# A written order for every engine in the late stage of an attention and FFN kernel

## The chip, the cores and the metric

The kernel runs on one core of one Trainium2 chip. The metric is the device time of one execution in microseconds (us). TensorE, the matrix engine, is PE in the profile, VectorE is DVE, ScalarE is ACT, GpSimd is POOL and SyncE, whose queue issues nearly all the transfers of this kernel, is SP.

## The reference

Windowed attention over 8 batches, 8 heads, 576 tokens and a head size of 64, and behind it a feed-forward network on the 4608 tokens, all in fp32:

```python
def _attn_ref(q, k, v):
    scores = scale * np.matmul(q, k.transpose(0, 1, 3, 2))
    ...
    scores = np.where(masks[None, :, :, :], scores, -1000000000.0)
    scores = scores - np.max(scores, axis=-1, keepdims=True)
    attn = np.exp(scores)
    attn = attn / (np.sum(attn, axis=-1, keepdims=True) + 1e-09)
    return np.matmul(attn, v)

def _moe_ref(x, w_in, w_out):
    h = x @ w_in                                                 # 4608x512 @ 512x2048
    g = np.maximum(h, 0.0) + np.log1p(np.exp(-np.abs(h)))        # softplus
    return g @ w_out                                             # 4608x2048 @ 2048x512
```

Half of the heads see the last 32 tokens, the other half every fourth of the last 128.

## The kernel before

**Chunks.** The 4608 tokens are taken in 9 chunks of 512 (`CH`). For each chunk the attention is computed in four groups of two heads (`Group`, numbered j = 0 to 3); their outputs, transposed, are the chunk's x (512 features by 512 tokens). Then come x @ w_in, softplus and the product with w_out. Fp32 products are made of three matmuls on fp32r parts: every operand is split into a high part (a cast, on ScalarE) and a low part (the value minus its high part, on VectorE).

**Three stages.** An opening, written out step by step by hand (`OPENING`), starts chunks 0 and 1; a middle stage does the rest of them in 32 slots, one tile of 128 hidden features by 512 tokens each (`h_part`, `o_part`). The late stage, chunks 2 to 8 (`FIRST = 2`), takes two hidden tiles at a time: it replaces the eight block products of a pair of tiles by seven, of sums and differences of blocks of x and of w_in. A chunk has 8 pairs (p0 to p7), and a pair has 7 steps (k0 to k6, the table `steps`). A step is one product of six matmuls 128x256 into one of two PSUM banks, h_x for k0, k2, k4, k6 and h_y for k1, k3, k5; then one sum on VectorE that takes the product out of PSUM (`aside`, lines 831 and 833; called "the aside" below); then `outputs`: one group of three matmuls 128x512 of the product with w_out, two groups after k6. The first two pairs of the late stage have 6 output groups each and not 8 (`between`), so the outputs run 12 groups behind: in the second pair (p1) of every chunk from 3 on, the four banks o_ps0 to o_ps3 get the last groups of the chunk before in k0 to k3, and the first groups of the new chunk in k4, k5 and, both, k6 (o_ps2, then o_ps3). Between those, the finished bank is copied out: o_ps1 and o_ps3 by ScalarE (line 865), o_ps0 and o_ps2 by VectorE (line 867).

**The other work of the late stage.** With a full hidden tile, ScalarE does Abs, Exp and Ln (lines 545 to 547, `activated`), VectorE the maximum with 0 and the sum (`softplus`, line 552), ScalarE the high part gh (line 567), VectorE the low part gl (line 573). The last tile halves of a pair come with the asides of k5 and k6. For the attention of the next chunk there are the scores on PE (s_ps), scaling, mask and maximum on VectorE (lines 347 and 350), eight exponentials on ScalarE (line 356), the divisor on VectorE (368, 371), the division on POOL (374), a transpose in squares on VectorE (407) whose result SP sends to DRAM and brings back in three pieces (turned<-squares, pt<-turned, line 132), and the values on PE (a_ps), copied to x_full by ScalarE (470). When a chunk's x is there, its block sums are made (`combine`, line 255) and the seven blocks are split into high and low parts (`split`, lines 270 and 271). In chunk 2, the last two of eight pairs of w_in tiles are converted to the late stage's form (`convert`, lines 696 to 714).

**Chunk 1's outputs** are accumulated in two runs. The sum of the first run is in DRAM (kept) and is loaded into ob tiles (line 590), which take the memory of chunk 2's block sums; the second run's PSUM banks are added to them (line 615) in p1 of chunk 2.

**What sets the order.** Matmuls and the loads made by `load_dma` keep the order of the program on their engines. So does all that goes through `pin` while `opening` is true, that is in the opening. Everywhere else the order on VectorE, ScalarE and POOL, and of the transfers issued with a plain `dma_start`, is chosen by the framework's scheduler from a simulated timeline. `at(when, ...)` puts a step of the attention or of the conversion into a list of events, and `pump(now)` issues those that are due. In the late stage one unit of `when` is one hidden tile, so a pair takes two.

## Time and profile before

| | |
|---|---|
| time, median of 3 runs | 907.86 us (906.24 to 909.62) |
| own time of the profiled execution | 907.07 us |
| its span, from the first to the last instruction | 905.3 us |
| PE busy | 879.8 us (97%) |
| VectorE busy | 634.9 us (70%) |
| ScalarE busy | 542.0 us (60%) |
| POOL busy | 64.1 us (7%) |
| mean granted clock of PE | 0.998 |
| first aside of the late stage / of chunk 8 | 238.48 us / 809.38 us |

The span is the time between the first and the last instruction; the execution's own time has what lies around it too. A row of the timeline gives the start of an instruction or of a run of like ones, how long it is busy, its engine, line, operation, the tiles it writes and reads, and their number; in brackets stands the idle time of the engine just before it and whose end it waited for. On PE matmuls overlap, so a matmul of 0.40 us may have the next one start 0.23 us after it. For SP the time is that of issuing; the data land later.

### The profile page before, as it was taken

The page shows a single profiled execution, that of the slowest core. Times are in us where ns is not written, and L with a number is a line of the kernel's source. Part 1 is how long each engine was busy: PE and PEld are TensorE (multiplying, and loading weights), DVE is VectorE, ACT ScalarE, POOL GpSimd, SP SyncE. Part 2 cuts the span into 40 slices and gives each one's busy share as a digit, 9 for nine tenths or more (in the row PEclk, how much of TensorE's full clock was granted, in tenths as well). Part 3 has the DMA queues.
Part 4 walks back from the last instruction along what each step waited for, and adds up shares of the span by engine and source line. Part 5 has one row for each costly group of instructions (what it writes and reads, how often), then busy time and mean ns, then how long its engine had stood idle before and what let it go on. Part 6 is the DMA issues. An engine that isn't in the chain of part 4 may idle for free.

```text
span 905.3 us, 18339 instructions
## 1 busy us (share of the span) xinstructions
PE 879.8 (97%) x6972; PEld 742.3 (82%) x6978; DVE 634.9 (70%) x1242; ACT 542.0 (60%) x1348; POOL 64.1 (7%) x46
## 2 busy tenths in 40 slices
PE   6899999999999999999999999999999999999998
PEld 3567888788788888888888888888888888889987
DVE  4799998997696586657666675668665866575444
ACT  6677677775555576556555665556555655564443
POOL 1320000000000000000000001000000000000000
PEclk9999999999999999999999999999999999999999
DMA  9989334333555546554555446545654455424223
GB/s 295 315 277 375 131 135 155 129 104 107 190 171 162 163 141 217 170 162 156 198 183 180 161 159 203 185 147 171 203 166 157 166 200 164 152 94 158 98 94 117
DMA packets 79095, 156.41 MB, mean 173 GB/s; under 512 B 8864, under 2 KB 21792, under 8 KB 79008
## 3 DMA queue, kind: packets, MB, share of 16 engines
q1 hardware_dynamic: 78432, 154.18, 51.2%
q8 instruction: 55, 0.90, 0.4%
q10 hardware_dynamic: 576, 1.07, 0.3%
q14 instruction: 32, 0.26, 0.1%
HBM read 124.28 MB, written 30.93 MB: 171 GB/s over the span
## 4 chain that ended last, share of the span: by engine, by line
PE 79%; DVE 12%; ACT 5%; DMA 2%; issue 2%; ACTq 0%; SPq 0%; DVEq 0%
PE o_ps L189 37%; PE h_x L189 17%; PE h_y L189 12%; PE h_ps L189 7%; PE a_ps L189 3%; ACT s L356 2%; PE s_ps L189 2%; DVE e L552 1%; DVE gl L573 1%; DVE s L347 1%; ACT e L547 1%; DMA k<-kpl 1%; DVE nm L350 1%; DMA out_t<-ob 1%; DVE a L162 1%
## 5 line engine op out<-in xcount | busy, mean ns | idle before, releaser
L189 PE MATMUL o_ps<-gh,t 128*128 128x512 f32 (+1 forms) x904 | 341.6, 391 | 0.0
L189 PEld LDWEIGHTS o_ps<-gh,t 128*128 128x128 f32 x904 | 169.7, 188 | 21.4
L189 PE MATMUL o_ps<-gl,t 128*128 128x512 f32 (+1 forms) x452 | 178.3, 394 | 0.0
L545 ACT ACTIVATE e<-hs 128x512 f32<-128x512 f32 x112 | 69.9, 629 | 162.2 <-DVE hs L833 160.7
L567 ACT CAST gh<-e 128x512 fp32r<-128x512 f32 x134 | 82.6, 617 | 65.7 <-DVE e L552 61.2
L552 DVE SCALAR_TENSOR_TENSOR e<-hs,e 128x512 f32<-128x512 f32 x112 | 76.4, 686 | 49.6 <-ACT e L547 49.5
L356 ACT ACTIVATE s<-s,nm 128x96 f32<-128x96 f32 x224 | 80.8, 362 | 48.9 <-DVE nm L350 48.6
L189 PEld LDWEIGHTS h_y<-s,t 128*128 128x128 f32 x672 | 94.6, 188 | 15.7 <-DVE temps L833 5.7
L374 POOL TENSOR_TENSOR s<-s,ri 128x768 f32<-128x768 f32 x36 | 56.9, 1580 | 699.1 <-ACT a L270 162.7
L189 PEld LDWEIGHTS h_x<-a,parts 128*128 128x128 f32 x672 | 92.5, 189 | 16.0 <-DVE hs L833 3.8
L189 PE MATMUL h_x<-a,parts 128*128 128x256 f32 x672 | 101.4, 287 | 2.6 <-DVE temps L831 1.3
L189 PE MATMUL h_y<-s,t 128*128 128x256 f32 x672 | 98.5, 282 | 3.8 <-DVE temps L833 3.6
L573 DVE TENSOR_TENSOR gl<-e,gh 128x512 fp32r<-128x512 f32 x144 | 97.5, 691 | 4.1 <-ACT gh L567 3.7
L546 ACT ACTIVATE e<-e 128x512 f32<-128x512 f32 x144 | 89.0, 625 | 2.1
L547 ACT ACTIVATE e<-e 128x512 f32<-128x512 f32 x144 | 88.4, 625 | 1.9
L189 PE MATMUL h_ps<-xh,parts 128*128 128x512 f32 x256 | 87.2, 397 | 2.2 <-DVE e L552 1.1
L833 DVE TENSOR_TENSOR hs<-h_x,temps 128x256 f32<-128x256 f32 x112 | 47.2, 421 | 59.9 <-PE h_x L189 59.1
L189 PEld LDWEIGHTS o_ps<-gl,t 128*128 128x128 f32 x452 | 86.1, 190 | 3.3 <-DVE gl L573 0.5
L189 PE MATMUL o_ps<-gh,parts 128*128 128x512 f32 x256 | 87.5, 394 | 0.0
L833 DVE TENSOR_TENSOR temps<-h_y,temps 128x256 f32<-128x256 f32 x112 | 46.8, 418 | 26.7 <-PE h_y L189 25.4
L189 PEld LDWEIGHTS h_ps<-xh,parts 128*128 128x128 f32 x256 | 48.1, 188 | 13.8 <-DVE e L552 1.6
L189 PEld LDWEIGHTS o_ps<-gh,parts 128*128 128x128 f32 x256 | 48.1, 188 | 10.3
(81 smaller groups left out, 1263.0 us busy)
## 6 DMA issues: line engine op xcount, KB each, us to landing
t<-w_out SPq DMA_DIRECT2D x224, 256.0 KB, 3.1
raw<-w SPq DMA_DIRECT2D x32, 512.0 KB, 10.1
v<-vp SPq DMA_DIRECT2D x36, 384.0 KB, 4.2
turned<-squares SPq DMA_DIRECT2D x28, 384.0 KB, 3.8
pt<-turned SPq DMA_DIRECT2D x84, 128.0 KB, 2.7
q<-qp SPq DMA_DIRECT2D x36, 256.0 KB, 3.5
w_out<-parts SPq DMA_DIRECT2D x16, 512.0 KB, 2.8
out_t<-ob SPq DMA_DIRECT2D x32, 256.0 KB, 2.1
```

The costliest lines, as they stand in the source:

```text
L162: pin(nc.vector.scalar_tensor_tensor(out=ai, in0=low, scalar=29, in1=ai, op0=ALU.logical_shift_right, op1=ALU.bitwise_or,))
L189: tc.keep_in_program_order(nc.tensor.matmul(**kw))
L347: nc.vector.scalar_tensor_tensor(out=dst, in0=src, scalar=1.0 / 8.0, in1=m, op0=ALU.mult, op1=ALU.add)
L356: pin(nc.scalar.activation(out=self.blocks[:, t], in_=src, func=AF.Exp, bias=self.nm[:, t : t + 1], scale=1.0 / 8.0 if self.masked else 1. ...
L374: pin(nc.gpsimd.tensor_tensor(out=self.blocks, in0=self.blocks, in1=self.ri.unsqueeze(2).to_broadcast([P, NB, WKEYS]), op=ALU.mult,))
L545: pin(nc.scalar.activation(out=e, in_=tiles[i], func=AF.Abs))
L546: pin(nc.scalar.activation(out=e, in_=e, func=AF.Exp, scale=-1.0))
L547: pin(nc.scalar.activation(out=e, in_=e, func=AF.Ln, bias=1.0))
L552: pin(nc.vector.scalar_tensor_tensor(out=e, in0=tiles.pop(i), scalar=0.0, in1=e, op0=ALU.max, op1=ALU.add))
L567: nc.scalar.copy(out=gh, in_=ready[i])
L573: pin(nc.vector.tensor_tensor(out=gl, in0=e, in1=gh.bitcast(F32), op=ALU.subtract))
L833: nc.vector.tensor_tensor(out=dst, in0=src, in1=temps[:, temp], op=ALU.add)
```

## The change

From chunk 2 on (`ordered = True` again before the loop over pairs) every instruction on VectorE, ScalarE and POOL and every outgoing transfer keeps the order of the program, and the program says in which step each stands. `step(n, k, ...)` gives an event the time of step k of pair n; events are kept in a heap. What is moved:

- Attention: the scores of a group stand at k5 of an even pair, the scaling and maximum at k6, the exponentials at k0 of the next pair, divisor and division at k4, the transpose at k6, the sending at k0 of the pair after that, the bringing at k3, the values a pair (for j = 0, some more) later. The first two groups of chunk 3 go through in the middle stage, at 26.7 and 29.7 (before 29.9 and 33.63).
- Softplus of the two tiles of a pair stands at k0 and k1 of the next pair, gh at k0 and k3, gl at k2 and k5.
- Splits: one high part and one low part per step from p7 to p0. The s1, a22 and s4 blocks of chunk 2, split before the loop until now, are split in its first pair.
- Block sums and the last conversions are "chores" in small pieces: a chore is taken at a step only if the sum of the costs so far, minus 1.41 for each step (2.11 for k6), leaves room (`behind`).
- A finished bank is copied one step (o_ps0, o_ps1) or two steps (o_ps2, o_ps3) after its last group (`finished`).
- The ob tiles of chunk 1 are loaded by an event in the last slot of the middle stage (`resumed_tiles`); the additions to them stand in steps of p1.

```diff
     def pin(ins):
-        if opening:
+        if ordered:
             tc.keep_in_program_order(ins)
...
+    def resumed_tiles(c):
+        for m in range(NKT):
+            ob_tile(m, True, c)
...
+    def step(n, k, part, *what, cost=0.0, after=0):
+        at(LATE + 2 * n + STEP * (k + 0.9) + 0.001 * after, part, *what, cost=cost)
...
+    def attend_late(n, pair, lag):
+        g = groups[n]
+        step(pair, 5, g.score, after=1)
+        step(pair, 5, load, n + 1, after=2)
+        step(pair, 6, g.maximum, cost=1.98)
+        step(pair + 1, 0, g.exponentials, after=3)
+        step(pair + 1, 4, g.divisor, cost=0.36)
+        step(pair + 1, 4, g.divide)
+        step(pair + 1, 6, turn, n, cost=0.97)
+        step(pair + 2, 0, send, n)
+        step(pair + 2, 3, bring, n)
+        step(pair + 2 + lag // 7, lag % 7, values, n, after=1)
...
+    at(LATE - 1, resumed_tiles, 1)
...
-    for name in ORDER[4:]:
-        split(FIRST, name)
+    ordered = True
...
-    def late_softplus(u):
+    def late_softplus(u, n):
         i = len(slots) + u
         tiles[i] = hs.pop(u)
         activated(i)
-        softplus(i)
-        g_high(i)
-        g_low(i)
+        second = u % 2
+        step(n + 1, second, softplus, i, cost=0.69, after=-12)
+        step(n + 1, 3 * second, g_high, i, after=-10)
+        step(n + 1, 5 if second else 2, g_low, i, cost=0.69)
...
-            dst = outs[0][:, m % 2]
-            if m % 2:
-                nc.scalar.copy(out=dst, in_=o_ps[m])
-            else:
-                nc.vector.tensor_copy(out=dst, in_=o_ps[m])
-            nc.sync.dma_start(out=out[m * P : (m + 1) * P, c * CH : (c + 1) * CH], in_=dst)
+            at(now[0] + (1 + m // 2) * STEP, finished, m, c, o_ps[m], cost=0.0 if m % 2 else 0.69)
...
             if k > 4:
-                late_softplus(u + k - 5)
-            if p == NPAIR - 1 and c + 1 < NCH:
-                split(c + 1, x)
+                late_softplus(u + k - 5, n)
+            now[0] = LATE + u + STEP * (k + 0.9)
             outputs(between.get(n, (1, 1, 1, 1, 1, 1, 2))[k])
-            pump(2 * NFF + u + 2 * (k + 1) / len(steps))
+            behind += pump(now[0] + 0.01) + ASIDE - (2.11 if k == 6 else 1.41)
+            while chores and chores[0][:2] <= (n, k) and behind + chores[0][2] < 0.4:
+                _, _, cost, chore = chores.pop(0)
+                chore()
+                behind += cost
+            behind = max(behind, 0.0)
```

Three places show what it does to the rows of an engine. The first is VectorE at the start of p1 of chunk 5, before the change. L831 and L833 are asides, L347 and L350 the masked scores and their maximum, L573 a gl, L867 the copies of o_ps0 and o_ps2.

```order
L347 SCALAR_TENSOR_TENSOR s_6169<-s_ps_6151,mask_5590 128x384
L347 SCALAR_TENSOR_TENSOR s_6169<-s_ps_6152,mask_5590 128x384
L573 TENSOR_TENSOR gl_6122<-e_6115,gh_6120 128x512
L831 COPY temps_2769<-h_x_2767 128x256
L573 TENSOR_TENSOR gl_6141<-e_6134,gh_6139 128x512
L867 COPY ob_4032<-o_ps0_5189 128x512
L350 TENSOR_REDUCE nm_6170<-s_6169 128x8
L833 TENSOR_TENSOR temps_2769<-h_y_2768,temps_2769 128x256
L831 COPY hs_6223<-h_x_2767 128x256
```

The same place with the change; asides are now L942 and L944, the maximum L365, the copies L960, and L571 is the softplus of a tile.

```order
L362 SCALAR_TENSOR_TENSOR s_6238<-s_ps_6198,mask_5409 128x384
L365 TENSOR_REDUCE nm_6239<-s_6238 128x8
L942 COPY temps_2835<-h_x_2833 128x256
L571 SCALAR_TENSOR_TENSOR e_6188<-hs_6143,e_6188 128x512
L944 TENSOR_TENSOR temps_2835<-h_y_2834,temps_2835 128x256
L571 SCALAR_TENSOR_TENSOR e_6226<-hs_6175,e_6226 128x512
L960 COPY ob_4078<-o_ps0_5251 128x512
L942 COPY hs_6304<-h_x_2833 128x256
L592 TENSOR_TENSOR gl_6309<-e_6188,gh_6254 128x512
L944 TENSOR_TENSOR temps_2835<-h_y_2834,temps_2835 128x256
```

Where a gl, a copy and the maximum stood between two asides, one or two pieces now stand.

The second place is ScalarE in the same pair, before the change: L567 gh, L865 the copies of o_ps1 and o_ps3, L356 the eight exponentials, L470 x_full, L545 and L546 the first steps of a tile's softplus.

```order
L567 CAST gh_6139<-e_6134 128x512
L865 COPY ob_4032<-o_ps1_5190 128x512
L356 ACTIVATE s_6169,sm_6174<-s_6169,nm_6170 128x96 x8
L865 COPY ob_4032<-o_ps3_5192 128x512
L470 COPY x_full_6261<-a_ps_6244 128x512
L545 ACTIVATE e_6287<-hs_6223 128x512
L545 ACTIVATE e_6306<-hs_6271 128x512
```

And with the change; the copies are L958, gh is L586, Abs, Exp and Ln are L564 to L566, and hs_6304 is the tile that the aside of k5 of this pair completes.

```order
L371 ACTIVATE s_6238,sm_6276<-s_6238,nm_6239 128x96 x8
L958 COPY ob_4078<-o_ps1_5252 128x512
L586 CAST gh_6325<-e_6226 128x512
L564 ACTIVATE e_6358<-hs_6304 128x512
L565 ACTIVATE e_6358<-e_6358 128x512
L566 ACTIVATE e_6358<-e_6358 128x512
L958 COPY ob_4078<-o_ps3_5254 128x512
L564 ACTIVATE e_6376<-hs_6336 128x512
```

The copy of o_ps3 stood ahead of the next tiles' Abs; it now stands behind the whole Abs, Exp and Ln of the tile that k5 completes.

The third place is SP around the start of the late stage, before the change. The t2 tiles are the first three tiles of w_out for the late stage, two loads each; ob<-kept are the loads for chunk 1's outputs, and turned and pt belong to the second attention group of chunk 3.

```order
L132 DMA t2_2069<-w_out_74 128x512
L132 DMA t2_2247<-w_out_74 128x512
L132 DMA t2_2335<-w_out_74 128x512
L132 DMA t2_2445<-w_out_74 128x512
L132 DMA t2_2552<-w_out_74 128x512
L132 DMA t2_2683<-w_out_74 128x512
L590 DMA ob_2850<-kept_73 128x512 x2
L590 DMA ob_2847<-kept_73 128x512 x2
L132 DMA turned_2786<-squares_2701 128x768
L132 DMA pt_2798<-turned_2786 32x4x256 x3
L623 DMA out_t<-ob_2847 128x512
```

The same queue with the change. ob_2772 takes the memory of the block sums from which s1 is split, ob_2775 that of those from which s4 is split; squares_2743 is made before the late stage.

```order
L609 DMA ob_2772<-kept_73 128x512 x2
L609 DMA ob_2775<-kept_73 128x512 x2
L133 DMA v_2825<-vp 96x1024
L133 DMA t2_2071<-w_out_74 128x512
L133 DMA t2_2247<-w_out_74 128x512
L133 DMA t2_2339<-w_out_74 128x512
L133 DMA t2_2446<-w_out_74 128x512
L133 DMA t2_2594<-w_out_74 128x512
L133 DMA t2_2731<-w_out_74 128x512
L133 DMA turned_2866<-squares_2743 128x768
L133 DMA pt_2892<-turned_2866 32x4x256 x3
L133 DMA out_t<-ob_2772 128x512
```

The loads of ob moved ahead of the six loads of w_out; the sending of the squares and the fetching of pt stand behind all of them, as a part of one queue.

On VectorE the low part of s4, on which ob_2775 waits, stands in the first pair of the late stage, behind the aside of k4 (the fifth L942 or L944 of the pair):

```order
L944 TENSOR_TENSOR temps_2835<-h_y_2834,temps_2835 128x256
L284 TENSOR_TENSOR a22_2854<-x_full_2221,a22_2854 128x512
L944 TENSOR_TENSOR hs_2903<-h_x_2833,temps_2835 128x256
L284 TENSOR_TENSOR s4_2868<-sums_2424,s4_2868 128x512
L944 TENSOR_TENSOR hs_2877<-h_y_2834,temps_2835 128x256
```

Before, it stood ahead of the first aside of the late stage:

```order
L271 TENSOR_TENSOR s4_2764<-sums_2456,s4_2764 128x512
L271 TENSOR_TENSOR s1_2758<-sums_2423,s1_2758 128x512
L407 STREAM_TRANSPOSE squares_2701<-s_2649 128x768
L271 TENSOR_TENSOR a22_2761<-x_full_2228,a22_2761 128x512
L573 TENSOR_TENSOR gl_2710<-e_2703,gh_2708 128x512
L831 COPY temps_2769<-h_x_2767 128x256
```

The splits of the three blocks moved from ahead of the loop to behind the asides of k1, k3 and k4.

More of the change, by code (lines that the diff above doesn't have):

```diff
@@ L1 @@
+import heapq
 import itertools
@@ L254, in combine @@
         )[n]()
-        nc.vector.tensor_tensor(out=dst[n], in0=a, in1=b, op=op)
+        out = dst[n]
+        if piece is not None:
+            out, a, b = (x[:, piece] for x in (out, a, b))
+        pin(nc.vector.tensor_tensor(out=out, in0=a, in1=b, op=op))
     ORDER = ("a11", "s2", "a12", "s3", "s1", "a22", "s4")
@@ L503, in values, with at @@
         load_v(n + 1)
-    events = []
-    def at(when, part, *what):
-        events.append((when, len(events), part, what))
+    events, serial = [], itertools.count()
+    def at(when, part, *what, cost=0.0):
+        heapq.heappush(events, (when, next(serial), cost, part, what))
     def send(n):
@@ L521, in pump @@
     def pump(now):
+        spent = 0.0
         while events and events[0][0] <= now:
-            _, _, part, what = events.pop(0)
+            _, _, cost, part, what = heapq.heappop(events)
             part(*what)
+            spent += cost
+        return spent
     STEPS = 2 * NKT
@@ L566, in g_high @@
         else:
-            nc.scalar.copy(out=gh, in_=ready[i])
+            pin(nc.scalar.copy(out=gh, in_=ready[i]))
         ready[i] = ready[i], gh
@@ L589, in ob_tile @@
         if resumed:
-            nc.sync.dma_start(out=obs[m], in_=kept[c, m])
+            pin(nc.sync.dma_start(out=obs[m], in_=kept[c, m]))
     def o_part(i, m):
@@ L611, in o_part @@
             )
-        if final:
+        if final and resumed and c:
+            at(now[0] + (2 + m // 2) * STEP, resumed_part, m, c, o_ps[m], cost=0.69)
+        elif final:
             src, dst = o_ps[m], obs[m]
@@ L738, in convert, with chores_of, homes_13, homes_2 @@
         weight_split_24(p)
+    def chores_of(p):
+        one = lambda: (homes[p][:, 0], homes[p][:, 1], diffs[p])
+        two = lambda: (*second(p), sums[p, 1][:, 1])
+        three = lambda: (*(wt[2 * p + 1, 0][:, part, :HALF] for part in range(2)), sums[p, 0][:, 1])
+        def homes_13():
+            homes[p] = const.tile([P, 2, 2, HALF], F32R, name="t13", tag=f"w{2 * p}_1")
+            weight_13(p)
+            high_part(*one())
+        def homes_2():
+            if p < NPAIR - 1:
+                rests[p] = const.tile([P, 2, 2, HALF], F32R, name="t2", tag=f"w{2 * p + 1}_1")
+            weight_24(p)
+            high_part(*two())
+            high_part(*three())
+        return [
+            (0.69, lambda: weight_sum(p, 0)), (0.69, lambda: weight_sum(p, 1)), (0.84, homes_13),
+            (0.84, homes_2), (0.69, lambda: low_part(*one())), (0.42, lambda: low_part(*two())),
+            (0.42, lambda: low_part(*three())),
+        ]
     def factors(p, name):
@@ L793, in tile_windowed_attention_softplus_ffn @@
+    for c in range(FIRST, NCH):
+        shares(c)
+    at(LATE - 1, resumed_tiles, 1)
     for i in range(OPENED + 1, len(slots)):
```

125 lines of the change are left out of this document (88 added, 37 removed).

## Prediction

> **What bounds the kernel now.** I read the page's first part and its chain, then what PE waits for, then the timeline of one place in chunk 5.
>
> ```profile
> span 905.3 us, 18339 instructions
> PE 879.8 (97%) x6972; PEld 742.3 (82%) x6978; DVE 634.9 (70%) x1242; ACT 542.0 (60%) x1348; POOL 64.1 (7%) x46
> PE 79%; DVE 12%; ACT 5%; DMA 2%; issue 2%; ACTq 0%; SPq 0%; DVEq 0%
> ```
>
> PE is busy nearly throughout. An order can win only the time in which PE waits, and the list of PE's waits says on whom it waits late in the kernel: on asides (VectorE's sums out of PSUM, L831 and L833).
>
> ```profile
> PE h_y L189 <- DVE temps L833: 3.8, 6, 0.7
> PE h_x L189 <- DVE temps L831: 1.3, 5, 0.3
> PE h_x L189 <- DVE hs L833: 1.1, 2, 0.7
> ```
>
> One such wait, at the start of p1 of chunk 5 (start, duration, engine):
>
> ```profile
> 536.28 1.02 DVE L347 SCALAR_TENSOR_TENSOR s<-s_ps,mask 128x384 f32<-128x384 f32 x2
> ...
> 538.74 0.68 DVE L867 COPY ob<-o_ps 128x512 f32<-128x512 f32 x1
> 539.34 0.94 DVE L350 TENSOR_REDUCE nm<-s 128x8 f32<-128x768 f32 x1
> 540.20 0.41 DVE L833 TENSOR_TENSOR temps<-h_y,temps 128x256 f32<-128x256 f32 x1
> 540.67 0.98 PE L189 MATMUL h_y<-s,t 128*128 128x256 f32 x6 [0.72 <-DVE temps L833]
> ```
>
> After the two scalings of the scores and other pieces VectorE copies a bank and takes the maximum, 1.5 us together, before it does the aside, and PE needs that bank: it stands for 0.72 us. That is what the change is about.
>
> How much of this there is in the late stage I get from the length of a pair in which nothing else happens, and of the whole stretch from the first aside of the stage to the first aside of chunk 8.
>
> ```profile
> 238.48 0.41 DVE L831 COPY temps<-h_x 128x256 f32<-128x256 f32 x1
> ...
> 809.38 0.42 DVE L831 COPY temps<-h_x 128x256 f32<-128x256 f32 x1 [0.76 <-PE h_x L189]
> ...
> 830.62 0.42 DVE L831 COPY temps<-h_x 128x256 f32<-128x256 f32 x1
> ...
> 841.16 0.42 DVE L831 COPY temps<-h_x 128x256 f32<-128x256 f32 x1
> ```
>
> A free pair (chunk 8 has no attention beside it) takes 841.16 − 830.62 = 10.54 us. The stretch of 48 pairs takes 809.38 − 238.48 = 570.90. Beside the pairs it holds the attention's matmuls:
>
> ```profile
> 533.80 0.39 PE L189 MATMUL o_ps<-gh,t 128*128 128x512 f32 x1
> ...
> 534.94 0.98 PE L189 MATMUL h_x<-a,parts 128*128 128x256 f32 x6
> ...
> 541.96 0.39 PE L189 MATMUL o_ps<-gh,t 128*128 128x512 f32 x1
> ...
> 543.36 0.98 PE L189 MATMUL h_x<-s,t 128*128 128x256 f32 x6
> ```
>
> Between these two pairs of rows lie one group's scores and one group's values. A w_out matmul is followed by the next after 0.23 us (two of them take 0.62 and the last of them 0.39, below), and a product behind attention takes 0.98 where one behind w_out takes 0.87 (below). So scores cost 1.14 − 0.23 + 0.11 = 1.02 and values 1.40 − 0.23 + 0.11 = 1.28. The stretch holds 23 scores (chunk 3's first are earlier) and 24 values, and its first two pairs have 4 output groups fewer, 0.70 each (three matmuls by 0.23). 48 × 10.54 − 2.8 + 23 × 1.02 + 24 × 1.28 = 557.1 (with the prices unrounded 557.05). **PE thus stands for 570.90 − 557.05 = 13.85 us in the late stage**; of the listed waits, 6.2 us are on asides. One step is (10.54 − 0.70) / 7 = 1.405 us, and k6 with its second group 2.11.
>
> **What goes.** An aside starts 0.91 us after its product (rows 836.59 and 837.50 below), is 0.42 long, and its bank is written again two products, 2.81 us, later; behind k6, whose bank k0 uses at once, the room is 2.11 − 1.33 = 0.78. One piece of up to 0.69 us beside an aside fits in every step; the scalings and the maximum (1.02 + 0.94, rows 536.28 and 539.34) stand after k6, with two steps' room. I followed the new row of VectorE through the steady pairs, p7 and p0 with the splits, and chunk 2 with its conversions, and found no step where the pieces exceed the room by more than some 0.1. I take all 13.85 off; if the cover fails at k6 of some pairs, each costs a few tenths, and I allow 1 us for all.
>
> **What comes: o_ps3.** PE's first matmul into o_ps3 for a new chunk stands in k6 of p1, and needs the bank copied out. That copy now stands on ScalarE behind Abs, Exp and Ln of the tile that k5's aside completes; queued behind it are the next tile's Abs, Exp and Ln. The same steps in chunk 8, where ScalarE is idle:
>
> ```profile
> 836.59 0.87 PE L189 MATMUL h_y<-a,parts 128*128 128x256 f32 x6
> ...
> 837.50 0.43 DVE L833 TENSOR_TENSOR hs<-h_y,temps 128x256 f32<-128x256 f32 x1 [0.98 <-PE h_y L189]
> ...
> 838.02 0.63 ACT L545 ACTIVATE e<-hs 128x512 f32<-128x512 f32 x1 [5.42 <-DVE hs L833]
> ...
> 838.68 0.63 ACT L546 ACTIVATE e<-e 128x512 f32<-128x512 f32 x1
> ...
> 839.17 0.62 PE L189 MATMUL o_ps<-gh,t 128*128 128x512 f32 x2
> ...
> 839.63 0.39 PE L189 MATMUL o_ps<-gl,t 128*128 128x512 f32 x1
> ```
>
> The second matmul of the row 839.17 is the first into o_ps3, at 839.40, 2.81 us after k5's product began. The copy's length is that of the group of such copies (0.577):
>
> ```profile
> L865 ACT COPY ob<-o_ps 128x512 f32<-128x512 f32 x12 | 6.9, 577 | 7.6 <-PE o_ps L189 7.6
> ```
>
> Abs, Exp and Ln follow each other by 838.68 − 838.02 = 0.66: they end at 838.02 + 3 × 0.66 = 840.00, the copy at 840.58, PE goes on some 0.05 later: 1.2 us late. Before, this copy stood right behind the exponentials, and no such wait is in PE's list. Chunks 3 to 8 each have such a p1: 6 × 1.2 = **7.2 us**. Ends: 0.9 each if ScalarE starts the three steps closer together, 1.45 with its restart and PE's: 5.4 to 8.7.
>
> **What comes: pt.** The values of chunk 3's second group stand in p1 of chunk 2, behind k1. They need pt, which comes by SP.
>
> ```profile
> 226.47 2.80 SPq L132 DMA_DIRECT2D t<-w_out  x6
> ...
> 235.92 1.75 SPq L590 DMA_DIRECT2D ob<-kept  x4
> ...
> 237.76 0.38 SPq L132 DMA_DIRECT2D turned<-squares  x1
> ...
> 242.55 1.27 SPq L132 DMA_DIRECT2D pt<-turned  x3
> ...
> 252.03 1.15 PE L189 MATMUL a_ps<-pt,v 96*64 96x64 f32 x32
> ```
>
> The page gives the three pieces 2.7 us to land:
>
> ```profile
> pt<-turned SPq DMA_DIRECT2D x84, 128.0 KB, 2.7
> ```
>
> Before, pt was issued at 242.55 and there by 246.1, 6 us ahead of the values. Now the queue holds first the loads into ob_2775, which wait for the low part of s4, behind k4's aside in the first pair. Counted from the start of that pair: k4's product begins at 4 × 1.405 = 5.6, its aside ends 1.34 later at 7.0, s4's low part at 7.6, the wait is seen at 7.7. Two loads of ob take 0.9 (1.75 for four), v 0.4, the six loads of w_out 2.8: turned is issued at 11.8. Its first fetch follows as before after 242.55 − 237.76 = 4.8, the third 0.85 later, and lands in 2.7: 20.1, and PE restarts at 20.2. PE would be there after the first pair (seven products of 0.70 and six groups of 0.70: 9.2), its scores (1.0) and k0 and k1 (2.8): 13.0. **PE stands 7.2 us**, and behind it q, k and the later loads are late too, but with pairs of room. Ends: 6 if turned lands in the page's usual time instead, 8.5 if the six loads of w_out slow it.
>
> **The clock after it.** A long wait of PE costs more than itself, as the opening of before shows:
>
> ```profile
> 20.00:24.00 4.00, 2.04 (x37) 1.27 (x36) 2.37 (x6) 2.75 (x16) 1.74 (x1) 0.99 1.04 363
> 24.00:27.00 3.00, 3.00 (x18) 1.20 (x18) 0.97 (x3) 2.13 (x4) 1.25 (x1) 0.50 1.06 267
> 27.00:30.00 3.00, 2.95 (x61) 2.09 (x58) 2.39 (x5) 1.02 (x2) 1.47 (x2) 0.94 1.02 341
> ```
>
> With PE busy 2.04 of 4 us, the granted clock falls to 0.50 for the next 3 and for 0.36 of the three behind (0.06 × 3 / 0.5): half of 3.36 is lost, 1.7. I take 1.5 (0 to 1.7). [...]
>
> **Small things.** At the start of the first pair a gl on VectorE stands ahead of k0's aside and waits for a gh that is now behind three casts of splits on ScalarE; together with the tail: 0.3 (0 to 1). The middle stage takes chunk 3's first groups earlier; PE has the same matmuls there, so I cost it at nothing, ±1.
>
> **Sum**, against the profiled execution's own 907.07: − 13.85 + 7.2 + 7.2 + 1.5 + 0.3 = 909.4. The median of the runs lies 0.79 above that execution, so 910.2. Ends of this case: all low 905.5, all high 914.
>
> **Rivals.** *No new wait*: if ScalarE and SP keep up, 907.07 − 13.85 + 0.79 = 894.0. For it speaks that PE's old waits were on VectorE alone; against it, that both new waits follow from the written order and rows of before. *Only one of the two*: with o_ps3 alone 894.0 + 7.2 + 0.3 = 901.5, if pt comes in time (squares that land in half the time, or a free s4 early); with pt alone 894.0 + 7.2 + 1.5 + 0.3 = 903.0, if ScalarE reaches the copy ahead of the tile.
>
> *Slower: VectorE is held by POOL's division.* The division of every group now stands at k4, and a gl at k5. In before one such meeting is seen:
>
> ```profile
> 427.31 0.64 DVE L271 TENSOR_TENSOR s<-sums,s 128x512 fp32r<-128x512 f32 x1
> ...
> 427.56 1.72 POOL L374 TENSOR_TENSOR s<-s,ri 128x768 f32<-128x768 f32 x1 [32.53 <-ACT a L270]
> ...
> 427.87 1.96 DVE L271 TENSOR_TENSOR a<-x_full,a 128x512 fp32r<-128x512 f32 x1
> ```
>
> The second low part, 0.64 before it, ends 0.55 after POOL, 1.3 late. [...] In the new order the division comes behind k4's aside (1.33 after the product) and the two pieces of the divisor:
>
> ```profile
> L371 DVE RECIPROCAL ri<-sm 128x8 f32<-128x8 f32 x36 | 7.2, 200 | 1.1
> L368 DVE TENSOR_SCALAR sm<-sm 128x8 f32<-128x8 f32 x36 | 6.1, 170 | 23.8 <-ACT s L356 23.7
> ```
>
> So it starts some 1.9 after k4's product (1.33 + 0.37 and a hand-over) and ends at 3.6; gl ends at 4.15, the aside of k6 at 4.5, and k0's product needs its bank at 4.9. With exponentials that end 0.5 later this tips, and every late of the 24 divisions can cost PE up to 0.4: at 0.15 on average 3.6 us, so 913.8. For it: the meeting is now certain at each odd pair; against it: the room of 0.4. It decides once gl ends 4.6 after k4's product.
>
> That the change doesn't do what it says can be ruled out from VectorE's row.
>
> **How the numbers follow.** My forecast's case has 0.52, no new wait 0.08, o_ps3 alone 0.09, pt alone 0.08, POOL's lock 0.23. A measurement of this kernel can tell about 0.5%, that is below 903.3 or above 912.4. Faster: 0.08 + 0.09 + half of pt alone = 0.21. Slower: the lock 0.23 and 0.03 of my own case's upper end: 0.26. Same: 0.53. The range takes in o_ps3 alone and the lock at its average: 901 to 914.5; left out are no new wait and the lock's upper half, under 0.2.
>
> **What would show it.** In the new profile: PE's waits on asides nearly gone; six waits of about 1.2 us of an o_ps matmul on ScalarE's copy (L958), in p1 of chunks 3 to 8; one wait of about 7 us of a_ps on the landing of pt, some 13 us into the late stage, with the clock at 0.50 behind it; and POOL's division beside a gl of about 2 us. Pairs 10.54 long between. The prediction is wrong if the copy of o_ps3 is done before k6, if pt lands before its values, or if waits on asides remain at several us.

## The result and the profile after

The changed kernel takes 914.17 us (median of 4 runs, 913.52 to 915.92) beside 907.55 for the kernel before (median of 4). The ratio is 1.0074, with a 95% interval of 1.005 to 1.0098: slower by 0.7%, with an interval that leaves out no change. The forecast was 910.2, the range 901 to 914.5; the result lies 0.3 us under its upper end. The profiled execution of the changed kernel is the longest of its four runs, 915.92.

The page of the changed kernel: the span, the busy time of the engines and the chain.

```profile
span 914.1 us, 18307 instructions
PE 880.1 (96%) x6972; PEld 747.8 (82%) x6978; DVE 644.0 (70%) x1257; ACT 552.9 (60%) x1348; POOL 65.0 (7%) x46
PE 81%; DVE 10%; ACT 4%; DMA 3%; issue 1%; SPq 0%; ACTq 0%; DVEq 0%
```

PE is as busy as before, 880.1 us for 879.8; the 8.8 us that the span grew are almost all time in which it stands. What it stands for is another matter than before (in total, times, longest):

```profile
PE a_ps L190 <- DMA pt<-turned: 9.0, 1, 9.0
PE o_ps L190 <- ACT ob L958: 5.7, 6, 0.9
...
PE o_ps L190 <- DVE ob L636: 1.8, 2, 0.9
```

The list has no wait on an aside any more (before, 6.2 us in the three lines that the prediction shows, and 0.3 in a fourth). In their place are the two waits that the prediction named, and a third, in the middle stage, that it did not.

The wait on ScalarE's copy, in p1 of chunk 5, from the timeline:

```profile
556.10 0.63 ACT L564 ACTIVATE e<-hs 128x512 f32<-128x512 f32 x1 [2.55 <-DVE hs L944]
...
557.43 0.63 ACT L566 ACTIVATE e<-e 128x512 f32<-128x512 f32 x1
...
557.97 0.57 ACT L958 COPY ob<-o_ps 128x512 f32<-128x512 f32 x1
...
558.59 0.50 PE L190 MATMUL o_ps<-gh,t 128*128 128x512 f32 x1 [0.95 <-ACT ob L958]
```

The row 556.10 says that ScalarE had stood idle for 2.55 us, because the next instruction in its written order was an Abs whose tile was not there yet. The last group of o_ps3 had ended at 554.85, so for half of that time the bank stood ready to be copied. Abs, Exp, Ln, then the copy: it ends at 558.54 and PE goes on at 558.59.

The wait for pt, from SP's, VectorE's and PE's rows:

```profile
247.37 5.11 SPq L609 DMA_DIRECT2D ob<-kept  x4
...
250.63 0.68 DVE L284 TENSOR_TENSOR s<-sums,s 128x512 fp32r<-128x512 f32 x1
...
253.00 2.81 SPq L133 DMA_DIRECT2D t<-w_out  x6
...
255.85 0.74 SPq L133 DMA_DIRECT2D turned<-squares  x1
...
262.30 1.27 SPq L133 DMA_DIRECT2D pt<-turned  x3
...
266.03 1.98 PE L190 MATMUL a_ps<-pt,v 96*64 96x64 f32 x32 [9.04 <-DMA pt<-turned]
```

The four loads of kept sums take 5.11 us to issue (1.75 before), because the last two stand until the low part of s4 ends at 251.31. Then the six loads, then the squares, whose data are there only 6.45 us after the issue (4.79 before). PE stands 9.04 us, and its a_ps then takes 1.98 us where it took 1.15: the clock. The windows around it have, after the span's length, PE's, PEld's, VectorE's, ScalarE's and POOL's busy time, the granted clock, DMA's share and GB/s:

```profile
257.00:266.00 9.00, 0.00 (x0) 0.00 (x0) 1.84 (x4) 3.24 (x17) 0.00 (x0) 0.68 0.74 256
266.00:269.00 3.00, 2.97 (x37) 2.88 (x38) 0.00 (x0) 0.95 (x2) 0.00 (x0) 0.50 0.53 185
269.00:272.00 3.00, 3.00 (x18) 2.88 (x18) 2.23 (x5) 0.15 (x1) 0.00 (x0) 0.75 0.70 218
```

PE works at half clock for 3 us and half of the next 3: 4.5 us, of which 2.2 are lost.

The third wait lies in the middle stage, at chunk 0's last outputs:

```profile
217.07 2.08 SPq L609 DMA_DIRECT2D ob<-kept  x2
...
221.85 0.69 DVE L636 TENSOR_TENSOR ob<-o_ps,ob 128x512 f32<-128x512 f32 x1 [1.23 <-DMA ob<-kept]
...
222.60 0.73 PE L190 MATMUL o_ps<-gh,parts 128*128 128x512 f32 x1 [0.95 <-DVE ob L636]
...
222.00:225.00 3.00, 2.40 (x6) 1.92 (x7) 3.00 (x5) 0.00 (x0) 0.00 (x0) 0.62 0.66 258
225.00:228.00 3.00, 3.00 (x13) 2.35 (x12) 2.50 (x6) 0.67 (x2) 0.00 (x0) 0.81 0.09 36
```

VectorE's addition waits 1.23 us for the load of the kept sum, and PE waits 0.95 us for the addition; a first such wait, of 0.86, ends 2 us earlier. Behind these two short waits the clock is at half for (1 − 0.62) × 2 × 3 + (1 − 0.81) × 2 × 3 = 3.4 us, another 1.7 lost.

### The profile page after: what moved, and what is told of

Read it like the earlier page. It is cut to its first block, busy times and chain, and to the rows that moved or that the text cites. A ratio compares the mean times of both kernels' runs of the same rounds, so it can differ in the third digit from the quotient of the medians.

```text
span 914.1 us, 18307 instructions
## 1 busy us (share of the span) xinstructions
PE 880.1 (96%) x6972; PEld 747.8 (82%) x6978; DVE 644.0 (70%) x1257; ACT 552.9 (60%) x1348; POOL 65.0 (7%) x46
## 4 chain that ended last, share of the span: by engine, by line
PE 81%; DVE 10%; ACT 4%; DMA 3%; issue 1%; SPq 0%; ACTq 0%; DVEq 0%
PE o_ps L190 39%; PE h_x L190 17%; PE h_y L190 13%; PE h_ps L190 5%; PE a_ps L190 4%; PE s_ps L190 2%; ACT s L371 2%; DVE a L168 1%; DVE a L163 1%; DMA k<-kpl 1%; DVE e L571 1%; DVE a L158 1%; DVE gl L592 1%; DVE a L154 1%; DMA turned<-squares 1%
## 5 line engine op out<-in xcount | busy, mean ns | idle before, releaser
L564 ACT ACTIVATE e<-hs 128x512 f32<-128x512 f32 x112 | 70.4, 629 | 203.2 <-DVE hs L944 202.9
L586 ACT CAST gh<-e 128x512 fp32r<-128x512 f32 x134 | 82.8, 618 | 70.6 <-DVE e L571 68.7
L592 DVE TENSOR_TENSOR gl<-e,gh 128x512 fp32r<-128x512 f32 x144 | 113.0, 785 | 3.7 <-ACT gh L586 3.2
L190 PEld LDWEIGHTS h_x<-a,parts 128*128 128x128 f32 x672 | 95.5, 190 | 10.1 <-DVE hs L944 0.3
L190 PE MATMUL h_x<-a,parts 128*128 128x256 f32 x672 | 98.6, 283 | 0.0
L565 ACT ACTIVATE e<-e 128x512 f32<-128x512 f32 x144 | 91.0, 632 | 4.2
L566 ACT ACTIVATE e<-e 128x512 f32<-128x512 f32 x144 | 91.0, 632 | 4.2
L944 DVE TENSOR_TENSOR hs<-h_x,temps 128x256 f32<-128x256 f32 x112 | 47.2, 421 | 64.2 <-PE h_x L190 64.2
L190 PE MATMUL o_ps<-gh,parts 128*128 128x512 f32 x256 | 89.4, 398 | 1.8 <-DVE ob L636 1.8
L944 DVE TENSOR_TENSOR temps<-h_y,temps 128x256 f32<-128x256 f32 x112 | 47.5, 425 | 58.9 <-PE h_y L190 58.6
L571 DVE SCALAR_TENSOR_TENSOR e<-hs,e 128x512 f32<-128x512 f32 x112 | 76.3, 681 | 1.8 <-ACT e L566 1.8
L190 PEld LDWEIGHTS a_ps<-pt,v 96*64 96x64 f32 x1152 | 39.0, 145 | 26.6 <-issue 19.8
```

The costliest lines, as they stand in the source:

```text
L190: tc.keep_in_program_order(nc.tensor.matmul(**kw))
L564: pin(nc.scalar.activation(out=e, in_=tiles[i], func=AF.Abs))
L565: pin(nc.scalar.activation(out=e, in_=e, func=AF.Exp, scale=-1.0))
L566: pin(nc.scalar.activation(out=e, in_=e, func=AF.Ln, bias=1.0))
L571: pin(nc.vector.scalar_tensor_tensor(out=e, in0=tiles.pop(i), scalar=0.0, in1=e, op0=ALU.max, op1=ALU.add))
L586: pin(nc.scalar.copy(out=gh, in_=ready[i]))
```

## The experiments

The theory: the order takes away the waits on asides as a whole, and the time comes back in waits that stand one beside the other: o_ps3 behind the softplus on ScalarE, pt behind the loads on SP, with the clock. The rivals: what is gained in one place is lost in another anyway (VectorE's backlog, POOL's division), so that taking one wait away brings another; and that it is not the steps of the order but the keeping of any order that counts. The medians below are from runs beside the kernel before on the same chip; it took 907.13 to 907.98 us in them, so a difference of less than 1 us between two versions says little.

**e1, the copy of o_ps3 one step earlier.**

```diff
-            at(now[0] + (1 + m // 2) * STEP, finished, m, c, o_ps[m], cost=0.0 if m % 2 else 0.69)
+            at(now[0] + (1 + (m == 2)) * STEP, finished, m, c, o_ps[m], cost=0.0 if m % 2 else 0.69)
```

> The changed kernel with one thing else: the copy of o_ps3 stands one step after its last group (k4) and no longer two (k5), so ahead of the softplus of the tile that k5 completes. If the six waits on ScalarE's copy are the cause of 6 x 1.21 us, they go and nothing takes their place: about 907 us (914.2 - 7.25), pairs of p1 fall from 12.85 to 11.64 long. Rival: the copy now waits for the ob half that o_ps1's copy used (its transfer has to land first), ScalarE stands in front of the softplus, and the wait moves to gh or to the bank: 911 to 914 us.

Measured: 907.57 us, 6.6 less than the changed kernel; ratio to the kernel before 0.9997 (0.9984 to 1.001). No wait on ScalarE's copy is left in PE's list. What the rival said is there, but has room:

```profile
551.38 0.59 ACT L958 COPY ob<-o_ps 128x512 f32<-128x512 f32 x1 [1.73 <-DMA out_t<-ob]
...
552.14 0.63 ACT L564 ACTIVATE e<-hs 128x512 f32<-128x512 f32 x1 [0.18 <-DVE hs L944]
```

The copy waits 1.73 us for the transfer out of the half that o_ps1's copy filled, and is done before the tile is there.

**e2, the loads of the kept sums behind pt.**

```diff
-    at(LATE - 1, resumed_tiles, 1)
+    step(0, 3, resumed_tiles, 1, after=3)
```

> The changed kernel with one thing else: the four loads of chunk 1's kept sums are issued in k3 of the late stage's first pair, behind the fetching of pt, and no longer ahead of it. If the wait of 9.1 us for pt comes from SP's queue standing before those loads, it goes, and with it the half clock behind it (about 1.2 us): 903 to 905 us. Rival: pt is late for another reason (the squares' transfer itself, contention with the six loads of w_out): the wait stays above 4 us and the time above 908. A second new wait is possible: the additions of the kept sums in the second pair then wait for their loads, 1 to 2 us.

Measured: 902.93 us, 11.2 less than the changed kernel; ratio to before 0.994 (0.9926 to 0.9955). The wait for pt is gone from PE's list; of the new waits the two others stand:

```profile
PE o_ps L190 <- ACT ob L958: 5.7, 6, 0.9
...
PE o_ps L190 <- DVE ob L636: 2.2, 2, 1.5
```

So the place of these loads in SP's queue was the cause of the 9 us and of the half clock behind them (mean granted clock of the profiled execution 0.995, 0.986 in the changed kernel).

**e3, both.**

> Both edits, the early copy of o_ps3 and the late loads of the kept sums. If the two costs stand side by side, they add: 914.2 - 7.25 - 10.3 = 896 to 898 us, which beats the kernel before by 1.1%. What would remain is the wait of chunk 0's last outputs in the middle stage (2 us and its half clock). Rival: with PE running ahead, VectorE or POOL's division becomes late and asides stall PE again: above 901 us.

Measured: 895.52 us; ratio to before 0.9859 (0.9843 to 0.9875). The two gains, 6.6 and 11.2, make 17.8, and both edits together bring 18.7: the costs stood side by side. The late stage of this kernel, from its first aside to the first of chunk 8:

```profile
240.25 0.88 PE L190 MATMUL h_x<-a,parts 128*128 128x256 f32 x6
...
242.17 0.42 DVE L942 COPY temps<-h_x 128x256 f32<-128x256 f32 x1
...
797.13 0.42 DVE L942 COPY temps<-h_x 128x256 f32<-128x256 f32 x1
```

554.96 us. By the prediction's own prices (its 557.05 less the 1.02 of one group's scores and the 1.28 of one group's values, which moved into the middle stage with chunk 3's first groups) a late stage without any wait takes 554.75. Of the 13.85 us of waits, 0.2 are left by this count; the row 240.25, the product that the first aside takes, is taken up below.

**e4, s1, a22 and s4 split ahead of the loop again.**

```diff
-    for c in range(FIRST, NCH):
+    for c in range(FIRST + 1, NCH):
         shares(c)
...
     pump(2 * NFF)
+    for name in ORDER[4:]:
+        split(FIRST, name)
     ordered = True
```

> The changed kernel with one part undone: the blocks s1, a22 and s4 of chunk 2 are split ahead of the loop, as before the change; the loads of the kept sums stay ahead of pt in SP's queue. If the queue stands only because ob's memory is freed by the low part of s4 in k4, this frees it about 8 us earlier and the wait for pt goes as with the late loads: 903 to 906 us, with some 1 us lost at the first pair where VectorE does the three low parts ahead of its first sum. Rival: the place in the queue alone decides: the wait stays above 5 us and the time above 909.

Measured: 906.13 us (902.73 to 909.45), 8.0 less than the changed kernel; ratio to before 0.9981 (0.9965 to 0.9997). Most of the wait goes, not all:

```profile
247.71 0.35 SPq L133 DMA_DIRECT2D turned<-squares  x1
...
254.62 1.27 SPq L133 DMA_DIRECT2D pt<-turned  x3
...
259.00 1.69 PE L190 MATMUL a_ps<-pt,v 96*64 96x64 f32 x32 [2.62 <-DMA pt<-turned]
```

The squares still stand behind eleven other loads (four of kept sums, one of v, six of w_out), and take 6.91 us to be there. The wait falls from 9.04 to 2.62, so the low part of s4 is most of the cause; the rest is that the squares are issued behind all these loads.

**e10, the six loads of w_out behind pt**, with the kept sums still ahead of it.

```diff
     for u in range(3):
-        load_w_out(u)
+        step(0, 3, load_w_out, u, after=5 + u)
```

> The changed kernel with the six loads of w_out put behind the sending and fetching of pt; the loads of the kept sums stay ahead of it. It splits the wait of 9.1 us: if 4.4 of it are the six loads (2.8 us to issue, and some 1.6 in which the squares' transfer stands behind their data), 4 to 5 us are left and the time is 908 to 910 us. Rivals: the kept sums' memory alone makes the wait: 8 us or more are left, 913 to 914; or the six loads alone: nothing left, 903.

Measured: 910.5 us, 3.7 less than the changed kernel; ratio to before 1.0033 (1.002 to 1.0045).

```profile
PE a_ps L190 <- DMA pt<-turned: 5.9, 1, 5.9
...
250.03 0.43 SPq L133 DMA_DIRECT2D turned<-squares  x1
...
256.08 1.27 SPq L133 DMA_DIRECT2D pt<-turned  x3
```

5.9 us are left where 4 to 5 were expected: the 2.8 us of issuing went, but the squares still need 6.05 us, only 0.4 less than in the changed kernel, where 1.6 had been put down to the six loads' data. Of the 9.0 us the six loads make some 3 by this edit, the wait for the memory some 6.4 by e4.

**e5, the order kept, without the steps**: the kernel before with every instruction of the late stage in the order in which its program is written.

```diff
     for name in ORDER[4:]:
         split(FIRST, name)
+    opening = True
```

(and `pin` around the late stage's instructions and transfers, as in the change).

> The kernel before with one part of the change alone: from chunk 2 on every engine keeps the order in which the program before is written, with none of the change's steps and times. If the gain of the change (13.85 us of waits on sums) lies in the steps and not in the keeping of an order, this is far slower: each of some 23 attention groups writes the divisor right behind the exponentials, VectorE stands about 3 us for ScalarE with sums queued behind it, of which the sum's room hides 1.4: 40 to 90 us more, 950 to 1000 us. Rival: the written order alone is good: 895 to 908 us.

Measured: 1264.96 us, ratio 1.3933 (1.3905 to 1.3961). The direction is as expected, the size far above it:

```profile
PE h_x L189 <- DVE hs L834: 170.7, 61, 7.8
PE h_x L189 <- DVE temps L832: 79.6, 36, 6.8
```

PE stands for asides 250 us in these two groups alone: not only the attention but each tile's softplus and chunk's splits, written in one piece, hold the asides behind them: a pair of chunk 8, which has no attention beside it, takes 14.68 us here and not 10.54. The mean granted clock is 0.908 (0.998 before).

**e6, the steps, without the order kept.**

```diff
     pump(2 * NFF)
-    ordered = True
```

> The changed kernel without keeping the order: the same steps and times in the program, the framework's scheduler orders VectorE, ScalarE and POOL in the late stage again. If keeping the order is needed, waits on sums come back, 5 to 15 us of them; the copy of o_ps3 is then no longer held behind the softplus (7 us less), and pt's wait depends on where the loads of the kept sums fall: 905 to 918 us. Rival: the program's times alone do it: no more than 2 us of waits on sums, 900 to 908 us.

Measured: 918.48 us, ratio 1.0117 (1.0094 to 1.0141), 0.5 above the upper end of what was expected. The waits on asides are back, the copy of o_ps3 and pt are not waited for:

```profile
PE h_x L190 <- DVE hs L943: 11.0, 18, 1.4
```

The 48 pairs from chunk 2 to chunk 7 take 576.14 us here, 21 more than in e3. Neither half of the change gains by itself. The order has to be kept, and it has to be one with steps.

**e8, the division at k5**, in e3's kernel.

```diff
-        step(pair + 1, 4, g.divisor, cost=0.36)
-        step(pair + 1, 4, g.divide)
+        step(pair + 1, 5, g.divisor, cost=0.36, after=-2)
+        step(pair + 1, 5, g.divide, after=-2)
```

> The third kernel (early copy, late loads) with the divisor and POOL's division moved from k4 to k5, ahead of a gl. If VectorE's gl, with two inputs in SBUF, is held until POOL's division ends, gl ends 3.9 to 4.1 us after k5's product, the sum of k6 at 4.3 to 4.4, and k0's product, due at 3.5, waits 0.8 to 1.0 in 22 pairs: 18 to 22 us more, 913 to 918 us. Rival (no lock between them): gl ends at 2.4 as ever, nothing waits: within 2 us of the third kernel.

Measured: 900.39 us, 4.9 above e3; ratio to before 0.9923 (0.9907 to 0.9939). Neither the 18 to 22 us nor nothing. In p7 of five chunks the mechanism is as expected:

```profile
519.18 0.64 DVE L284 TENSOR_TENSOR a<-x_full,a 128x512 fp32r<-128x512 f32 x1
519.43 1.72 POOL L389 TENSOR_TENSOR s<-s,ri 128x768 f32<-128x768 f32 x1 [21.66 <-DVE ri L386]
...
519.73 1.96 DVE L592 TENSOR_TENSOR gl<-e,gh 128x512 fp32r<-128x512 f32 x1
...
522.17 0.95 PE L190 MATMUL h_x<-a,parts 128*128 128x256 f32 x6 [0.90 <-DVE hs L944]
```

The gl that begins 0.30 after the division ends 0.54 behind its end, and PE waits 0.90 for the aside of k6; the list has five such waits, 4.5 us. In the other 17 pairs the gl is first:

```profile
543.66 0.64 DVE L592 TENSOR_TENSOR gl<-e,gh 128x512 fp32r<-128x512 f32 x1
...
543.92 1.72 POOL L389 TENSOR_TENSOR s<-s,ri 128x768 f32<-128x768 f32 x1 [22.77 <-DVE ri L386]
```

There gl takes its 0.64, the division runs 1.72 where it takes 1.47 when it starts first (row 555.69 below), and nothing on PE waits. In these rows the one that starts first holds the other up: gl takes 1.96 us for 0.64, the division 1.72 for 1.47. The price of 0.8 to 1.0 was right; that all 22 pairs would pay it was wrong, since the instruction that VectorE has behind the divisor starts before the division does (543.66 and 543.92). In 17 pairs that instruction is the gl; in p7 it is the low part of a split (row 519.18), and the gl comes second, behind the division's start.

**e7, chunk 3's first groups behind chunk 0's outputs**, and **e9, the conversions earlier**, in e3's kernel: two attempts at the third wait, neither of which took it away.

```diff
-                attend(c, j, (26.7, 29.7)[j], (0.5, 2.8, 3.2, (5.0, 4.8)[j]))
+                attend(c, j, (28.2, 30.2)[j], (0.5, 2.8, 3.2, (5.0, 4.8)[j]))
```

> The third kernel (early copy, late loads) with chunk 3's first two groups scored at 28.2 and 30.2 in the middle stage and no longer at 26.7 and 29.7, behind chunk 0's last outputs. If the two waits of 2 us in all for chunk 0's additions, and the half clock behind them, come from that group's VectorE work delaying the conversion that frees ob's memory, they go: 2 to 3.5 us less than the third kernel, 892 to 894 us. Rival: the conversion is late anyway: within 1 us of the third kernel.

```diff
-        at(20.5 + 1.9 * p, convert, p)
+        at((19.0, 20.7, 22.4, 24.1, 25.6, 29.0)[p], convert, p)
```

> The third kernel (early copy, late loads) with the first five conversions of w_in pairs begun 1.5 to 4.4 slots earlier in the middle stage (the sixth 1 earlier). Chunk 0's additions wait for loads whose memory a conversion still holds; with the conversions done by then, the two waits of 2 us and the half clock behind them go: 2 to 3.5 us less than the third kernel's 895.5, 892 to 894 us. Rival: the earlier conversions crowd VectorE elsewhere in the middle stage, and another wait of 1 us or more takes their place: 895 us or more.

Measured: 896.99 us for e7 (ratio to before 0.9882, 0.9866 to 0.9899), 1.5 above e3; 906.04 us for e9 (0.9978, 0.9952 to 1.0003), 10.5 above it. (The edit of e9 begins the first five conversions 1.5 to 2.5 slots earlier, not up to 4.4.) In e7 one wait of 2.1 us on chunk 0's additions is left, and its ratio's interval overlaps that of e3. In e9 the loads of the kept sums come latest of all:

```profile
220.34 3.17 SPq L609 DMA_DIRECT2D ob<-kept  x3
...
223.86 0.47 PE L190 MATMUL o_ps<-gh,parts 128*128 128x512 f32 x1 [2.79 <-DVE ob L636]
```

Its fifth conversion stands right ahead of chunk 0's outputs and takes the same memory as the ob tiles. PE's list has 5.7 us of waits on the additions (2.0 in e3) and another new one of 2.9 on a pt, and a matmul of 128x512 takes 0.63 us from 227.1 to 235.5 (0.40 at 224.4 and 236.2), as in the changed kernel at a granted clock of 0.50 (0.63 at 223.1), so the 10.5 us are not the additions alone. This fits the idea of the memory, but it only makes the wait longer and does not take it away; so the conversions were split around the outputs.

**e11, the last three conversions behind chunk 0's outputs**, in e3's kernel.

```diff
-        at(20.5 + 1.9 * p, convert, p)
+        at((20.5, 22.4, 24.3, 28.0, 29.2, 30.4)[p], convert, p)
```

> The third kernel (early copy, late loads) with the last three conversions of the middle stage put behind chunk 0's last outputs (28.0, 29.2 and 30.4, before 26.2, 28.1 and 30), so that no conversion holds the memory of chunk 0's ob tiles when their loads are due. If that memory is the cause of the 2 us of waits on chunk 0's additions, the loads are issued well ahead of the additions, the waits and the half clock behind them go: 2 to 3.5 us less than the third kernel's 895.5, 892 to 894 us. Rival: the loads are late for another reason (the scheduler's place for them, VectorE's backlog): within 1 us of the third kernel; or the last conversions crowd the start of the late stage: 896 us or more.

Measured: 893.9 us (892.94 to 894.51); ratio to before 0.985 (0.9834 to 0.9867).

```profile
203.41 2.19 SPq L609 DMA_DIRECT2D ob<-kept  x3
...
PE h_x L190 <- DVE temps L942: 0.4, 1, 0.4
```

Three of the four loads are issued 9 us ahead of the additions, the fourth 3 us ahead; no addition is waited for, and the one wait on VectorE that is left behind the opening is 0.4 us. So a conversion that holds the ob tiles' memory made the third wait. The gain over e3, 1.6 us, is a little less than expected: e3's profiled execution had the two waits (2.0 us) but, by the time to the next q load (5.10 us for 6.73 in the changed kernel, below), not the half clock behind them. By the times alone the gain is not clear of noise, as the two intervals overlap; that the waits are gone is what the trace shows. This version has the lowest median, 13.7 us under the kernel before.

## Why the prediction was right, and where it was off

**What went.** Right: no wait on an aside is left in the list of the changed kernel, and 13.7 of the 13.85 us are gone in e3. That only 0.2 us seem to be left comes from the count. In the kernel before and in e3 the first aside of the late stage comes 1.9 to 2.0 us after the start of its product (236.50 and 240.25) and not 0.91 as in a steady pair, so a stretch that begins with it is 1.0 too short. Counted from the product, the kernel before has some 14.9 us of waits and e3 still some 1.2, of which its list names 0.8 (0.5 on pt, 0.3 on an aside); the gain is the same. The list of before names only about half of these waits; what the others were it does not say. That the steps and the kept order are both needed was not argued in the prediction; e5 and e6 show it.

**o_ps3.** Right: 6 waits in p1 of chunks 3 to 8, 7.2 us by the sum. The list has 5.7 us of idle time; by length, p1 of chunks 3 to 7 takes 12.85 us in the changed kernel and 11.64 to 11.67 in e1, that of chunk 8 11.75 and 10.54, which makes 7.1 for the six. The median of e1 is 6.6 us lower.

**pt.** Right in cause, too small in size: 7.2 against 9.0. Counted from the start of the first pair (its product at 243.75), PE came to the place when forecast (13.1 us for 13.0), and the squares were issued 0.3 us late (12.1 for 11.8). The mis-sized term is the time from the issue of the squares to the first fetch. I took 4.8, as before; it was 6.45. I had kept a slower transfer as the upper end of the term (8.5) and not as the value, and the wait lies above that end too. That the six loads of w_out alone slow it, as I had put it there, is not shown: with them behind the squares, in e10, it is still 6.05, behind four kept sums and a v. With a v and the six loads ahead it is 6.72 in e2 and 7.66 in e3, and with all eleven 6.64 in e1 and 6.91 in e4. It is longer with more loads ahead, but not by their number alone; what sets it stays open.

**The clock.** 1.5 against 2.2 behind pt: the half clock held for 4.5 us of work, not 3.4. The lower end of 0 no run shows: behind a wait for pt of 2.62 us, in e4, a_ps still takes 1.69 us and the product behind it 1.65 (1.15 at 240.43 and 0.98 at 251.79 in the same trace). In the middle stage two waits, of 0.86 and 0.95 us, 1 us apart, were followed by 3.4 us of half clock (0.50 in each us from 223 to 226). Not every short wait was: around the six on ScalarE's copy, of up to 0.95 us and each by itself, the granted clock is 1.00 (from 271 to 911 us). Nor does the fall show in e3 and e10, with waits on the additions like those of the changed kernel (2.0 us in two, 2.1 in three). The next q load is issued 5.10 and 5.11 us behind that of the squares there, in the changed kernel 6.73 (223.46 to 230.19, where the scores ahead of it end at 230.10); the 1.6 between them is, by my estimate, the half clock that e3 and e10 did not have. It is a risk of a short wait, not a fixed price.

**The middle stage.** This step failed: "I cost it at nothing, ±1". It gained some 1.3 us (the wait of h_ps on VectorE's softplus, 1.1 in the list of before, is gone) and lost 2.0 in the two waits on chunk 0's additions and 1.7 in the clock behind them. Before:

```profile
PE h_ps L189 <- DVE e L552: 1.1, 1, 1.1
...
201.17 0.42 DVE L704 TENSOR_TENSOR t<-b 128x256 f32<-128x256 f32 x1
...
203.49 3.73 SPq L590 DMA_DIRECT2D ob<-kept  x3
...
236.50 0.88 PE L189 MATMUL h_x<-a,parts 128*128 128x256 f32 x6
```

After, with what SP waits for between 195 and 232 us:

```profile
209.90 0.41 DVE L736 TENSOR_TENSOR t<-b 128x256 f32<-128x256 f32 x1
...
243.75 0.88 PE L190 MATMUL h_x<-a,parts 128*128 128x256 f32 x6
...
SPq L609 <- DVE t L748: 4.3, 2, 2.6
```

The late stage's first product starts 7.25 us later; 2.3 of it is a longer opening, 2.3 the scores and values that moved into the middle stage, and 2.7 are left, where these terms make 2.4. I had looked at PE's matmuls there, which are the same, and not at the memory that the conversions share with chunk 0's ob tiles (one pool of three buffers). The fourth conversion (L704, after L736) ran at 201.17 before and at 209.90 after, 6.5 us later without the opening's part; the loads, which wait for its low parts (L748), were issued from 203.49 before and from 213.14 after. e11, where this conversion comes behind the additions, shows that it is this memory. Why VectorE comes to the conversion so late stays open. The scores of chunk 3 in the same slots are not enough: in e7, which moves them behind, it starts no earlier (208.28, in e3 207.96).

**The sum again** with what was measured, from 907.07: − 13.65 (13.85 less 0.2) + 7.1 for o_ps3 + 9.0 + 2.2 − 1.3 + 2.0 + 1.7 = 914.1; the median is 914.17. That it fits to the tenth is luck: it leaves out smaller differences, such as the end of the kernel, which takes 0.8 us longer from the last pair's first aside on. (In the prediction the prices as printed add up to 557.3 and not 557.1; the difference is rounding.) The profiled execution of the changed kernel, 915.92, was longer because its opening, in which no instruction moved, took 2.3 us more than that of the profile of before.

**The rivals.** No new wait, and only one of the two, fell: both are there, and e1 to e3 show what each is worth. VectorE held by POOL's division, the lock of the prediction's chances, is there, but inside the room:

```profile
555.69 1.47 POOL L389 TENSOR_TENSOR s<-s,ri 128x768 f32<-128x768 f32 x1 [23.40 <-DVE ri L386]
...
555.92 1.78 DVE L592 TENSOR_TENSOR gl<-e,gh 128x512 fp32r<-128x512 f32 x1
...
557.63 0.41 DVE L944 TENSOR_TENSOR hs<-h_x,temps 128x256 f32<-128x256 f32 x1
```

The gl of k5 takes 1.78 in place of 0.69; the aside of k6 follows at once and ends at 558.04, and PE waits for no aside. In e1, where o_ps3 no longer gives VectorE time, there is none either. The prediction's room of 0.4 was enough, and e8 shows what happens when it is not. There both sides show: gl takes 1.96 us when the division started ahead of it, the division 1.72 when gl did.

So the kernel came out slower by 0.7% and not within 0.5%, since pt, its clock and the middle stage were 1.8, 0.7 and 2.4 us dearer than the sum had them. The case that came true is the one forecast, with a third wait that it did not have. That the time still lies in the range is partly luck: these three terms lie above their own upper ends (8.5, 1.7 and 1), and it is the room that the range left for o_ps3, up to 8.7, that made up for part of it.

## What to carry to other kernels

A written order takes away the waits that a scheduler leaves and makes new ones where an instruction that is ready stands behind one that is not: go through each engine's row, and for every instruction whose result another engine needs, ask what is ahead of it that is not ready yet. Do that for the DMA queue too, where a load that waits for its memory holds up all behind it (here four loads took 5.11 us to issue, 1.75 before), and where the time from an issue to the first fetch of its data can be longer than at another place (here 6.45 us, 4.79 before). Here two lines (a copy one step earlier, four loads behind three) turned 0.7% of loss into 1.4% of gain.

## What the runs showed of the hardware beside that

VectorE and POOL held each other up by who started first: in e8 a gl took 1.96 us in place of 0.64 when it began 0.30 behind the division, and the division took 1.72 in place of 1.47 when the gl was first. The granted clock fell behind two waits of 0.9 us in the changed kernel (0.62 and 0.81 in the two windows behind them), and stayed at 1.00 around the six waits of up to 0.95 us on ScalarE's copy. And the time from the issue of the squares' transfer to the first fetch behind it was 4.79 us behind four kept sums (before), 6.05 behind four kept sums and a v (e10), 6.45 to 6.91 behind eleven loads (the changed kernel, e1, e4), but 6.72 and 7.66 behind a v and the six loads of w_out (e2, e3).
